# Output projection and MLP of a transformer block: products on pairs of 16-bit floats in place of fp32r pairs, with the MLP weights split once

## The chip, the cores and the metric

The kernel runs on one core of a Trainium2 chip. The metric is the device time of one execution in microseconds (us); the times of a kernel are given as the median of several runs. A core has TensorE (PE in the profile, its weight loads as PEld), VectorE (DVE), ScalarE (ACT), GpSimd (POOL) and SyncE (SP), which issues the DMAs here. Each engine works through its own instructions in order; semaphores tie them together.

## The reference

One pre-norm transformer block over S = 2048 rows of D = 512: softmax attention with 32 heads of 16, and an MLP with F = 1792 and SiLU. All inputs and the output are float32.

```
qkv = layernorm(x) @ wqkv
p   = softmax(q @ k.T / 4)            # 32 heads of 16
h   = x + concat(p @ v) @ wo
out = h + silu(layernorm(h) @ w1) @ w2
```

## The kernel before, in words

The kernel wants nearly float32 precision from matmuls on cheaper operands. It splits each operand into a high part and a rest ("low") and adds three products, high by high, low by high and high by low (`product`, L123). In the projections of q, k and v, the output projection and the MLP, both parts are of the type fp32r, a 4-byte type. The queries and keys, once projected, are pairs of 16-bit floats instead: `measure` (L454) finds a power of two from the sums of squares of the weights, so that nothing overflows, and `project_qk` (L468) scales and splits with it.

Time has these stages.

- **Projections** (to about 188 us in the profile). In units of one product (12 matmuls, `project_qk`, `project_v` L492) over four blocks of 512 rows; the last 24 units run in a loop over groups of heads (L661). ACT copies the result out of PSUM, scaled, POOL takes the rest, and SP stores q and k to DRAM (`qd`, `kd`). Two or three PSUM banks serve the products in turn.
- **Attention**. The loop at L1109 goes over 512 groups: 4 blocks of 512 queries x 8 items (four heads each) x 16 key chunks. A group has four score matmuls (`scores`, L400), ACT's four exponentials, and eight matmuls for the values of two groups before (`values`, L689). Softmax needs the maximum of each row of scores ahead of time; `maximum` (L245) makes a matmul of 48 rows into a PSUM bank and a DVE reduction, 64 per item. A planner (`maxima`, L1087) places up to three per group and the rest elsewhere: `burst` (L379) puts several at fixed steps of other products. The maxima and other work share three banks that are taken in turn (L677), and at times the bank `pv`.
- **Small chains beside it**: `finish_max` (L261) on DVE and POOL and `place_max` (L291) turn maxima into rows of the queries; `sums`, `invert`, `spread`, `divide` (L769 to L794) divide the attention output by its sums through DRAM, with POOL's slow power operation in `invert`. `soon` (L317) queues such a step some groups ahead.
- **Output projection** of a finished block (`output`, L946, in the first item of the next block): `split_rows` (L832) splits the rows, `project_rows` (L852) multiplies, then statistics, normalisation and transposes.
- **MLP** (`mlp`, L894): 14 steps over F in chunks of 128. A step has a first product with w1 (12 matmuls into `pv`), `gate` (L867: SiLU and cast on ACT, the rest `gl` on DVE) and the second product with w2 of the chunk before (`second`, L874: 12 matmuls into four accumulating banks). Bursts of 3, 3 and 4 maxima stand at steps 5 and 12 of the first product and 8 of the second (`BESIDE_C`, L74); the third block has none in its last three steps (`QUIET`, L78), the fourth none at all. The first three blocks' MLPs run this way between groups of attention.
- **The last block** (`finish_last`, L980) has its output projection and MLP in an order written out by hand.

The weight tiles of the MLP are loaded and split anew in each block: `load_weights` (L813) loads 128 x 512 float32, and `split_weights` (L821) casts the high part on ACT and takes the rest on POOL, or on DVE in the last block:

```
w = raw_w.pop((kind, f))
...
act("copy", wh, w)
...
low(wl, w, wh, engine)
```

Of the kernel before, what the change touches and what calls it, by code (L numbers as in the profile page):

```python
# [20 lines left out]
P = 128  # L21
# [14 lines left out]

TOP = 2.0 ** 15
MX = 2.0 ** 15

# [42 lines left out]
def attention_mlp_kernel(ctx: ExitStack, tc: tile.TileContext, x, wqkv, wo, w1, w2, out):  # L82
# [28 lines left out]
    def low(dst, src, high, engine="dve"):  # L111

        if engine == "pool":
            pool("tensor_tensor", dst, src, high.bitcast(F32), ALU.subtract)
        else:
            dve("tensor_tensor", dst, src, high.bitcast(F32), ALU.subtract)

# [34 lines left out]
    nc.vector.tensor_copy(ident_h, ident)  # L152
    expo = const.tile([P, 1], F32, name="expo")
    nc.gpsimd.memset(expo, -0.5)
    minus = const.tile([P, 16], F32, name="minus")
# [3 lines left out]
    qk_s = const.tile([P, 1], F32, name="qk_s")  # L159
    qk_e = const.tile([P, 1], F32, name="qk_e")  # L160

    fix_q = const.tile([16, 512], F16, name="fix_q")
# [12 lines left out]

    def statistics(rows):
# [6 lines left out]
        pool("tensor_scalar", rs, mv[:, 1:2], EPS, None, op0=ALU.add)  # L183
        pool("tensor_tensor", rs, rs, expo, ALU.pow)
        return mv, rs
# [226 lines left out]
    with ExitStack() as pa:  # L412
# [15 lines left out]
        scaled = ks[RING - 1].rearrange("p a n -> p (a n)").bitcast(F32).rearrange("p (t n) -> p t n", n=512)  # L428
        scaled = [scaled[:, t, :] for t in range(4)]
        flat = va.rearrange("p c h d -> p (c h d)")  # L430
# [7 lines left out]

        sq = small.tile([P, NG], F32, name="sq", bufs=1)

        def square(n):
# [26 lines left out]
        def project_qk(b, n, beside={}, scale=False, kind="st"):  # L468
# [9 lines left out]
            if scale:  # L478

                t = scaled[b]  # L480
# [94 lines left out]
        for t in range(4):  # L575
# [18 lines left out]
        for b in range(NB):  # L594
# [3 lines left out]
            for n, (kind, k) in enumerate(units + vs if b else units):  # L598
                tick()
                rows, (stats, norms, turns) = None, ((), (), ())  # L600
                if b + 1 < NB:
                    rows = xts[b + 1]
                    stats, norms, turns = (other_ln if b else first_ln)[n]

                def layer_norm():
                    for t in stats:
                        found[t] = statistics(rows[:, t, :])
                    for t in norms:
                        normalize(rows[:, t, :], rows[:, t, :], *found.pop(t), engine="pool" if kind == "v" else "dve")
# [74 lines left out]
    ot = [cpool.tile([P, 4, DC, P], F32, name=f"ot{i}") for i in range(2)]  # L684
    wo_h = cpool.tile([P, DC, D], F32R, name="wo_h")
    wo_l = cpool.tile([P, DC, D], F32R, name="wo_l")
    hth = cpool.tile([P, DC, 512], F32R, name="hth")
    htl = cpool.tile([P, DC, 512], F32R, name="htl")
    def values(g):  # L689
# [55 lines left out]
    def divide_part(part, pvs, o_t, kind="st"):  # L745
# [3 lines left out]
        halves = ps.rearrange("p t (m j r) -> p t m j r", m=2, r=32)[:, :, :, :, :DH + 1]  # L749
        both = gp.tile([P, 4, P], F32, name="both", tag="ol")[:, :, :2 * (DH + 1)].rearrange("p t (j r) -> p t j r", j=2)  # L750
# [3 lines left out]
        dve("reciprocal", rc, both[:, :, :, DH])  # L754
        to = o_t[:, :, 64 + 32 * part:96 + 32 * part].rearrange("p t (j d) -> p t j d", j=2)
        dve("tensor_tensor", to, both[:, :, :, :DH], rc[:, :, :, None].to_broadcast([P, 4, 2, DH]), ALU.mult)
# [17 lines left out]
    def invert(i):  # L774
# [4 lines left out]
        pool("tensor_tensor", x, x, rc, ALU.mult)  # L779
        pool("tensor_scalar", x, x, -1.0, 2.0, op0=ALU.mult, op1=ALU.add)  # L780
        pool("tensor_tensor", rc, rc, x, ALU.mult)
# [25 lines left out]

    raw_w, ws, hx, os = {}, {}, {}, {}


    first_weights = {9: ("w1", 0), 12: ("w1", 1), 14: ("w2", 0), 15: ("w1", 2)}

    def load_weights(kind, f):  # L813
        if f < FC:
            w = raw_w[kind, f] = gp.tile([P, 512], F32, tag="w", name="w", bufs=4)
            if kind == "w1":
                dma(w.rearrange("p (c n) -> p c n", n=P), w1[:, f * P:(f + 1) * P].rearrange("(c p) n -> p c n", p=P))
            else:
                dma(w, w2[f * P:(f + 1) * P, :])

    def split_weights(kind, f, engine, high="act", pt=False):  # L821
        if f < FC:
            w = raw_w.pop((kind, f))
            wh, wl = ws[kind, f] = [pt_tile(kind + part, F32R) if pt else gp.tile([P, 512], F32R, name=kind + part)
                                    for part in "hl"]
            if high == "act":
                act("copy", wh, w)
            else:
                dve("tensor_copy", wh, w)
            low(wl, w, wh, engine)  # L830

    def split_rows(b, t, chunks=slice(None)):  # L832
        if chunks.start != DC - 1:
            os[t] = [gp.tile([P, DC, P], F32R, name=name) for name in ("oh", "ol")]
        (h, l), o = (x[:, chunks] for x in os[t]), ot[b % 2][:, t, chunks]
# [6 lines left out]

    def split_wo(c, w):
        pool("tensor_copy", wo_h[:, c, :], w)
        low(wo_l[:, c, :], w, wo_h[:, c, :], "pool")
# [14 lines left out]
    def add_rows(b, t, ps):  # L860

        dve("tensor_tensor", rows_of(b, t), ps, hx[t], ALU.add)

    def turn_rows(t):
        turn(hx.pop(t), hth[:, :, t * P:(t + 1) * P], htl[:, :, t * P:(t + 1) * P])

    def gate(ps, engine="dve"):  # L867
        g, gh, gl = (pt_tile(name, dt) for name, dt in (("g", F32), ("gh", F32R), ("gl", F32R)))
        act("activation", g, ps, AF.Silu)
        act("copy", gh, g)  # L870
        low(gl, g, gh, engine)
        return gh, gl

    def second(b, acc, f, gh, gl, inserts={}):  # L874
# [8 lines left out]
        for t, step in enumerate(steps):  # L883
# [5 lines left out]
            for m in range(parts):  # L889
                cols = slice(m * D // parts, (m + 1) * D // parts)  # L890
                dve("tensor_tensor", h[:, cols], acc[t][:, cols], h[:, cols], ALU.add)
                dma(out[n * P:(n + 1) * P, cols], h[:, cols])

    def mlp(b):  # L894
# [10 lines left out]
        for f in range(FC):  # L905
# [21 lines left out]
            parts = gate(ps, "dve" if f else "pool")  # L927
            if f == FC - 1:
# [17 lines left out]
    def output(b, n):  # L946
# [13 lines left out]
        if n < 4:  # L960
            found[n] = statistics(rows_of(b, n))

# [17 lines left out]
    def finish_last(pending):  # L980
# [22 lines left out]
        def add(t):  # L1003
            h = rows_of(b, t)
            dve("tensor_tensor", h, ps_rows[t], hx[t], ALU.add)
            found[t] = statistics(h)

# [23 lines left out]

        split_weights("w1", 2, "dve", pt=True)
        some(1, 5)
# [24 lines left out]
        turn_second(3)  # L1058
        split_weights("w2", 0, "dve")
        for f in range(3):  # L1060
            begin(f, 1)
        acc, waiting = [], []
        for f in range(FC):
# [10 lines left out]
            waiting.append((f, *gate(ps)))  # L1074
            if f:
                split_weights("w1", f + 2, "dve")
            if f > 1:
                split_weights("w2", f - 1, "dve")
            if f > 1:
                second(b, acc, *waiting.pop(0))  # L1080
        split_weights("w2", FC - 1, "dve")
        while waiting:
# [26 lines left out]
    for g in range(groups):  # L1109
# [7 lines left out]
        if g < DC:  # L1117
            w = gp.tile([P, 512], F32, tag="w", name="w", bufs=4)
            dma(w, wo[g * P:(g + 1) * P, :])
            soon(8, split_wo, g, w)  # L1120
        if i in FIRSTS:
            b, n = i // 8 - 1, c - OUTPUT
# [10 lines left out]
            if c == 13:  # L1133
                split_weights("w1", 0, "pool")
        if i == LAST:
# [5 lines left out]
            if c == 4:  # L1141
                for f in range(3):
                    load_weights("w1", f)
                load_weights("w2", 0)
                for f in range(2):
                    soon(8 + f, split_weights, "w1", f, "dve", "dve")
        if g == 1:
# [64 lines left out]
```

## Time and profile before

| | |
|---|---|
| median of 3 runs | 1664.33 us (1663.91 to 1664.33) |
| span of the profiled execution | 1662.2 us; some 2 us of the run's time lie around it |
| projections | to about 188 us |
| MLP of the first block | from about 486 us, some 110 us |
| MLP of the last block | 1588 to 1657 us |
| DMA | 102.85 MB, 62 GB/s on average |

The profile has one execution. Its page gives the busy time of each engine, then groups of instructions by source line, engine, operation and tile: `out<-in`, partitions x elements and type, count, busy time in us and mean ns of one, idle time before and what ended it. fp32r operands show as f32 in matmul rows and as fp32r where an engine writes them. Timeline rows give start, duration, engine, line, operation, tiles and count; rows that follow one another are merged. Matmuls overlap in a pipeline, so a matmul's duration isn't its cost; the distance from one start to the next is. Helpers such as `mm` (L89), `act` (L103), `dve` (L106) and `pool` (L96) record all operations of an engine, so tiles tell the groups apart.

### The profile page before, as it was taken

What the parts mean: (1) busy time and instruction counts of PE and PEld (TensorE: products, weight loads), DVE (VectorE), ACT (ScalarE), POOL (GpSimd) and SP (SyncE); (2) the same over time, 40 slices, a digit from 0 to 9 for tenths busy, and PEclk for the clock granted to TensorE, in tenths of its full rate; (3) what the DMA queues carried; (4) which work ended last, traced back from release to release, by engine and by line L of the source; (5) the groups of instructions that cost most, each with busy time, mean ns of one, the idle gap of its engine ahead of it and who ended that gap; (6) DMA issues with size and microseconds to landing.
All of it is one profiled execution on the core that took longest, in us unless ns stands there. A gap on an engine that the chain in (4) does not pass through costs nothing.

```text
span 1662.2 us, 28571 instructions
## 1 busy us (share of the span) xinstructions
PE 1649.9 (99%) x10551; PEld 649.6 (39%) x10551; DVE 1454.3 (87%) x2403; ACT 1235.3 (74%) x2435; POOL 397.3 (24%) x584
## 2 busy tenths in 40 slices
PE   9999999999999999999999999999999999999999
PEld 7666422222245532222245532222245632222387
DVE  7899999999988889999988889999978769999443
ACT  5323799999953389999962379999962389999743
POOL 5423311211234301211244311211235311111100
PEclk9999999999999999999999999999999999999999
DMA  5434411211232111111232111121232211100222
GB/s 201 107 98 143 119 32 37 58 32 37 72 73 67 58 50 35 42 50 33 60 76 79 58 50 32 37 58 32 61 70 76 68 50 34 33 12 21 65 77 82
DMA packets 104409, 102.85 MB, mean 62 GB/s; under 512 B 22737, under 2 KB 81169, under 8 KB 104269
## 3 DMA queue, kind: packets, MB, share of 16 engines
q1 hardware_dynamic: 104268, 101.02, 22.4%
q8 instruction: 83, 1.36, 0.4%
q14 instruction: 58, 0.47, 0.1%
HBM read 77.72 MB, written 17.29 MB: 57 GB/s over the span
## 4 chain that ended last, share of the span: by engine, by line
PE 90%; DVE 5%; ACT 3%; issue 1%; POOL 0%; DMA 0%; DVEq 0%; POOLq 0%; ACTq 0%
PE pv L89 35%; PE ps_s L89 21%; PE ps_m L89 11%; PE ps_acc L89 10%; PE ps_qk L89 5%; PE ps_w L89 3%; DVE mx L257 3%; PE ps_v L89 3%; ACT pt L103 2%; PE ps_wo L89 2%; PE ps_tr L92 1%; DVE st L106 0%; DVE pvs L106 0%; DVE hx L106 0%; PE ps_n L92 0%
## 5 line engine op out<-in xcount | busy, mean ns | idle before, releaser
L257 DVE TENSOR_REDUCE mx<-ps_m 128x1 f32<-128x512 f32 x2011 | 1261.7, 684 | 80.8 <-PE ps_m L89 50.6
L103 ACT ACTIVATE pt<-ps_s 128x512 f32<-128x512 f32 x2048 | 1010.7, 608 | 31.9 <-PE ps_m L89 17.4
L89 PE MATMUL pv<-pt,va 128*17 128x512 f32 x4096 | 537.6, 598 | 0.9
L89 PE MATMUL ps_s<-qs,ks 64*128 64x512 f16 x2048 | 532.2, 379 | 2.0 <-ACT pt L103 0.6
L89 PE MATMUL ps_m<-ks,qs 48*128 48x512 f16 x2011 | 504.8, 380 | 0.7 <-DVE mx L257 0.2
L89 PEld LDWEIGHTS <-ks 64*128 64x128 f16 x2048 | 150.2, 95 | 548.1 <-issue 435.4
L96 POOL TENSOR_TENSOR ri<-rc,minus 128x16 f32<-128x16 f32 x31 | 90.8, 2928 | 305.8 <-DMA rc<-dn 305.8
L89 PEld LDWEIGHTS pv<-pt,va 128*17 128x17 f32 x4096 | 69.0, 95 | 215.0 <-issue 202.3
L89 PEld LDWEIGHTS <-qs 48*128 48x128 f16 x2048 | 119.2, 94 | 62.6 <-issue 56.7
L103 ACT CAST w2h<-w 128x512 fp32r<-128x512 f32 x56 | 34.7, 619 | 99.6 <-PE ps_acc L89 99.6
L103 ACT ACTIVATE g<-pv 128x512 f32<-128x512 f32 x39 | 23.3, 597 | 100.1 <-PE pv L89 100.1
L89 PE MATMUL ps_acc<-w2l,gh 128*128 128x512 f32 x224 | 92.6, 413 | 0.0
L89 PE MATMUL ps_acc<-w2h,gh 128*128 128x512 f32 x224 | 92.0, 411 | 0.0
L96 POOL TENSOR_TENSOR w2l<-w,w2h 128x512 fp32r<-128x512 f32 x42 | 53.9, 1284 | 147.9 <-ACT w2h L103 147.9
L89 PE MATMUL ps_acc<-w2h,gl 128*128 128x512 f32 x224 | 88.6, 396 | 0.0
L106 DVE TENSOR_TENSOR gl<-g,gh 128x512 fp32r<-128x512 f32 x53 | 37.3, 703 | 56.2 <-ACT gh L103 56.2
L103 ACT ACTIVATE ks<-ps_qk,qk_s 128x512 f32<-128x512 f32 x30 | 20.7, 689 | 68.8 <-PE ps_qk L89 66.9
L96 POOL TENSOR_SCALAR nm<-nm 128x16 f32<-128x16 f32 (+1 forms) x50 | 12.8, 255 | 232.7 <-DVE nm L268 229.7
L89 PE MATMUL pv<-htl,w1h 128*128 128x512 f32 x156 | 65.5, 420 | 0.0
L89 PE MATMUL pv<-hth,w1h 128*128 128x512 f32 x156 | 62.4, 400 | 0.1
L89 PE MATMUL pv<-hth,w1l 128*128 128x512 f32 x156 | 61.4, 393 | 0.0
L96 POOL TENSOR_TENSOR w1l<-w,w1h 128x512 fp32r<-128x512 f32 x42 | 54.3, 1292 | 11.3 <-ACT w1h L103 11.3
(138 smaller groups left out, 1396.3 us busy)
## 6 DMA issues: line engine op xcount, KB each, us to landing
w<-in_B_w_dram SPq DMA_DIRECT2D x112, 256.0 KB
ks<-kd SPq DMA_DIRECT2D x120, 192.0 KB
qs<-qd SPq DMA_DIRECT2D x128, 48.0 KB
kd<-sh SPq DMA_DIRECT2D x16, 256.0 KB
qd<-sh SPq DMA_DIRECT2D x16, 256.0 KB
hx<-in_A_x_dram SPq DMA_DIRECT2D x16, 256.0 KB
ot<-pvs SPq DMA_DIRECT2D x124, 32.0 KB
den<-dr SPq DMA_DIRECT2D x124, 32.0 KB
```

The source lines that it names most:

```text
L89: tc.keep_in_program_order(nc.tensor.matmul(*a, **k))
L92: tc.keep_in_program_order(nc.tensor.transpose(*a))
L96: tc.keep_in_program_order(getattr(nc.gpsimd, op)(*a, **k))
L103: pin(getattr(nc.scalar, fn)(*a, **k))
L106: pin(getattr(nc.vector, fn)(*a, **k))
L257: pin(nc.vector.tensor_reduce(mx[piece][:, j, a % n, qt, kb:kb + 1], ps, axis=AX.X, op=ALU.max))
```

## The change

- The operands of the output projection, of the first MLP product and of the second (`wo_h`, `wo_l`, `hth`, `htl`, w1, w2, `gh`, `gl`, the split rows) become pairs of 16-bit floats. The three products stay three, with the same counts and sizes. The projections of q, k and v stay on fp32r.
- So that 16-bit floats hold them, w1, w2, wo, the attention output and the gate are scaled by powers of two. They are found on the chip: during the projections SP loads w1, w2 and wo in 32 pieces of 128 x 512, ACT squares each with an accumulated sum (`square_rest`), and squares the value weights in one instruction (`square_values`); then one small matmul and small operations of DVE and POOL make the factors (`measure_rest`, `set_factors`). The staging takes two of the four `scaled` buffers of `project_qk`. The layer norm of the MLP scales its rows by 1024.
- The factors are taken out again in operations that are there anyway: the residual adds become operations with a scalar factor, SiLU takes a scale, the cast of the gate becomes a multiplication, and `gl` an operation with a scalar factor, always on DVE.
- w1 and w2 are split once: from group 12 of attention, every fourth group loads one of 28 tiles; four groups later POOL scales it, a group later casts it, another group later takes the rest, and SP stores the pair to DRAM (`wd`). In the MLPs `load_weights` loads the finished pair, in the same number of bytes. `split_weights` in its old form goes, with all its calls, and `split_wo` has one more POOL operation.

```diff
+        def square_rest(u):
+
+            n = u - 4
+            if 0 <= n < len(pieces):
+                act("activation", staged[n % 2], staged[n % 2], AF.Square, accum_out=rest_sq[:, n:n + 1])
+            n = u - 2
+            if 0 <= n < len(pieces):
+                dma(staged[n % 2], pieces[n])
...
+                square_values()
...
             for n, (kind, k) in enumerate(units + vs if b else units):
                 tick()
+                square_rest(2 + 6 * (b - 1) + n if b else n)
...
                 n = 8 * g + m - 12
+                square_rest(n + 24)
+                if n == 14:
+                    measure_rest()
+                if n == 16:
+                    set_factors()
...
     def load_weights(kind, f):
         if f < FC:
+            w = parts_of(raw_tile())
+            dma(w, wd[kind][f])
+            ws[kind, f] = w[:, 0], w[:, 1]
...
+    def split_weights(kind, f, w):
+
+        parts = parts_of(raw_tile())
+
+        def store():
+            low(parts[:, 1], w, parts[:, 0], "pool")
+            dma(wd[kind][f], parts)
+
+        pool("tensor_scalar", w, w, w1_s if kind == "w1" else w2_s, 1.0, op0=ALU.mult, op1=ALU.mult)
+        soon(1, lambda: pool("tensor_copy", parts[:, 0], w))
+        soon(2, store)
...
-        act("copy", gh, g)
-        low(gl, g, gh, engine)
-        return gh, gl
+    def gate(ps):
+        g, parts = pt_tile("g"), parts_of(pt_tile("gh"))
+        act("activation", g, ps, AF.Silu, scale=h_f)
+        act("mul", parts[:, 0], g, g_s)
+        dve("scalar_tensor_tensor", parts[:, 1], g, g_s, parts[:, 0], op0=ALU.mult, op1=ALU.subtract)
+        return parts[:, 0], parts[:, 1]
...
-            for kind, n in (("w2", f), ("w1", f + 1)) if f else (("w1", 1), ("w2", 0)):
-                split_weights(kind, n, "pool")
...
+        f, c4 = divmod(g - SPLIT, 4)
+        if c4 == 0 and 0 <= f < 2 * FC:
+            kind, f = ("w1", "w2")[f % 2], f // 2
+            soon(4, split_weights, kind, f, load_raw(kind, f))
```

More of the change, by code (lines that the diff above doesn't have):

```diff
@@ L37 @@
 TOP = 2.0 ** 15
+LN = 2.0 ** 10
+BOUND = 23.0
+PIECES = 14, 14, 4
+SPLIT = 12
 MX = 2.0 ** 15
@@ L111, in low @@
     def low(dst, src, high, engine="dve"):
[L113 to L116, printed above, removed]
+        if high.dtype == F32R:
+            high = high.bitcast(F32)
+        (pool if engine == "pool" else dve)("tensor_tensor", dst, src, high, ALU.subtract)
     def run(*parts):
@@ L160, in attention_mlp_kernel @@
     qk_e = const.tile([P, 1], F32, name="qk_e")
+    factors = const.tile([P, 14], F32, name="factors")
+    sigma, inverse = factors[:, :4], factors[:, 4:8]
+    w1_s, w2_s, wo_s, o_s = (sigma[:, n:n + 1] for n in range(4))
+    h_f, g_s, out_f, wo_f, o_minus, o_twice = (factors[:, n:n + 1] for n in range(8, 14))
     fix_q = const.tile([16, 512], F16, name="fix_q")
@@ L174, in attention_mlp_kernel, with statistics @@
     dr = dram.tile([H, 4, 512], F32, name="dr")
-    def statistics(rows):
+    wd = {kind: dram.tile([FC, P, 2, 512], F16, name=f"{kind}d") for kind in ("w1", "w2")}
+    def statistics(rows, scale=1.0):
         st = small.tile([P, 6], F32, name="st", bufs=5)
@@ L428, in attention_mlp_kernel @@
         scaled = ks[RING - 1].rearrange("p a n -> p (a n)").bitcast(F32).rearrange("p (t n) -> p t n", n=512)
-        scaled = [scaled[:, t, :] for t in range(4)]
+        scaled, staged = ([scaled[:, t, :] for t in half] for half in ((0, 1), (2, 3)))
         flat = va.rearrange("p c h d -> p (c h d)")
@@ L439, in attention_mlp_kernel, with square_values, measure_rest, set_factors @@
         sq = small.tile([P, NG], F32, name="sq", bufs=1)
+        free = qs[RING - 1].rearrange("p a n -> p (a n)").bitcast(F32)
+        rest_sq, norms = free[:, :sum(PIECES) + 1], free[:, 64:68]
+        pieces = [w.rearrange("(p r) f -> p (r f)", p=P)[:, 512 * n:512 * (n + 1)]
+                  for w, count in zip((w1, w2, wo), PIECES) for n in range(count)]
+        def square_values():
+            act("activation", ks[RING - 1].rearrange("p a n -> p (a n)").bitcast(F32).rearrange(
+                "p (c n) -> p c n", n=512), raw_v, AF.Square, accum_out=rest_sq[:, sum(PIECES):])
+        def square_rest(u):
[5 more added lines that the diff above has]
+                dma(staged[n % 2], pieces[n])
+        def measure_rest():
+            n = sum(PIECES)
+            ps = bank("ps_sq", "sm")
+            mm(ps[:, :n + 1], ones, rest_sq, start=True, stop=True)
+            dve("tensor_reduce", norms[:, :2], ps[:, :28].rearrange("p (a k) -> p a k", a=2), axis=AX.X, op=ALU.add)
+            dve("tensor_reduce", norms[:, 2:3], ps[:, 28:n], axis=AX.X, op=ALU.add)
+            dve("tensor_copy", norms[:, 3:4], ps[:, n:n + 1])
+            pool("tensor_scalar", norms, norms, 1e-30, None, op0=ALU.add)
+            pool("tensor_tensor", norms, norms, expos, ALU.pow)
+        def set_factors():
+            dve("tensor_scalar", sigma[:, :3], norms[:, :3], TOP, None, op0=ALU.mult)
+            dve("tensor_scalar", sigma[:, 3:], norms[:, 3:], TOP / BOUND, None, op0=ALU.mult)
+            dve("tensor_scalar", sigma.bitcast(U32), sigma.bitcast(U32), 0x7F800000, None, op0=ALU.bitwise_and)
+            dve("reciprocal", inverse, sigma)
+            for to, a, f in ((h_f, inverse[:, :1], 1 / LN), (g_s, w1_s, 1 / 32.0), (o_minus, o_s, -1.0),
+                             (o_twice, o_s, 2.0), (out_f, inverse[:, :1], 32.0)):
+                pool("tensor_scalar", to, a, f, None, op0=ALU.mult)
+            pool("tensor_tensor", out_f, out_f, inverse[:, 1:2], ALU.mult)
+            pool("tensor_tensor", wo_f, inverse[:, 2:3], inverse[:, 3:], ALU.mult)
         def square(n):
@@ L478, in project_qk @@
             if scale:
-                t = scaled[b]
+                t = scaled[b % 2]
                 act("mul", t, ps, qk_s)
@@ L684, in attention_mlp_kernel @@
     ot = [cpool.tile([P, 4, DC, P], F32, name=f"ot{i}") for i in range(2)]
[L685 to L688, printed above, removed]
+    wo_h = cpool.tile([P, DC, D], F16, name="wo_h")
+    wo_l = cpool.tile([P, DC, D], F16, name="wo_l")
+    hth = cpool.tile([P, DC, 512], F16, name="hth")
+    htl = cpool.tile([P, DC, 512], F16, name="htl")
     def values(g):
@@ L805, in split_half, with raw_tile, parts_of, load_raw @@
         low(l, o, h)
-    raw_w, ws, hx, os = {}, {}, {}, {}
+    ws, hx, os = {}, {}, {}
     first_weights = {9: ("w1", 0), 12: ("w1", 1), 14: ("w2", 0), 15: ("w1", 2)}
+    def raw_tile():
+        return gp.tile([P, 512], F32, tag="w", name="w", bufs=8)
+    def parts_of(w):
+        return w.bitcast(F16).rearrange("p (s n) -> p s n", s=2)
     def load_weights(kind, f):
         if f < FC:
[L815 to L830, printed above, removed]
+            w = parts_of(raw_tile())
+            dma(w, wd[kind][f])
+            ws[kind, f] = w[:, 0], w[:, 1]
+    def load_raw(kind, f):
+        w = raw_tile()
+        if kind == "w1":
+            dma(w.rearrange("p (c n) -> p c n", n=P), w1[:, f * P:(f + 1) * P].rearrange("(c p) n -> p c n", p=P))
+        else:
+            dma(w, w2[f * P:(f + 1) * P, :])
+        return w
+    def split_weights(kind, f, w):
[6 more added lines that the diff above has]
+        soon(2, store)
     def split_rows(b, t, chunks=slice(None)):
         if chunks.start != DC - 1:
-            os[t] = [gp.tile([P, DC, P], F32R, name=name) for name in ("oh", "ol")]
+            parts = gp.tile([P, 2, DC, P], F16, name="oh")
+            os[t] = parts[:, 0], parts[:, 1]
         (h, l), o = (x[:, chunks] for x in os[t]), ot[b % 2][:, t, chunks]
@@ L1058, in finish_last @@
         turn_second(3)
-        split_weights("w2", 0, "dve")
         for f in range(3):
```

46 lines of the change are left out of this document (18 added, 28 removed).

## The prediction

> **What bounds the kernel now.** I read the head of the page first, then the chain that ended last, then the busy time by stretches, then the timeline of one stretch.
>
> ```profile
> span 1662.2 us, 28571 instructions
> PE 1649.9 (99%) x10551; PEld 649.6 (39%) x10551; DVE 1454.3 (87%) x2403; ACT 1235.3 (74%) x2435; POOL 397.3 (24%) x584
> PE 90%; DVE 5%; ACT 3%; issue 1%; POOL 0%; DMA 0%; DVEq 0%; POOLq 0%; ACTq 0%
> ```
>
> PE carries 90% of the chain. A busy PE says little, so the question by stage is how far apart its matmuls start, and which engine would be late if they came closer. In the rows by stretches below, the columns are the stretch, its length, then PE, PEld, DVE, ACT and POOL busy, the granted clock, the DMA share and GB/s. The four are the projections, attention, ten steps of the first block's MLP, and the last block's MLP.
>
> ```profile
> 100.00:150.00 50.00, 50.00 (x242) 30.91 (x241) 48.81 (x82) 17.35 (x29) 19.53 (x32) 1.00 0.52 149
> 300.00:400.00 100.00, 99.76 (x766) 22.41 (x765) 95.86 (x158) 99.85 (x204) 16.56 (x29) 1.00 0.17 42
> 500.05:577.78 77.73, 77.69 (x341) 46.03 (x341) 68.52 (x111) 23.59 (x40) 30.73 (x34) 1.00 0.22 67
> 1588.76:1656.23 67.47, 67.47 (x292) 54.71 (x292) 23.43 (x37) 27.00 (x48) 0.00 (x0) 1.00 0.25 79
> ```
>
> An MLP step of the first three blocks takes 7.77 us (77.73 / 10). ACT works 2.36 us of it and POOL 3.07, so the weight splits that the change takes from them are hidden there. DVE works 6.85, so only 0.92 us per step is slack. In the last block DVE is busy a third of the time, and PE alone sets the pace.
>
> **Part 1: the matmuls.** These are the groups by shape of the third matmul of each product, each standing for three groups of equal count:
>
> ```profile
> L89 PE MATMUL ps_acc<-w2h,gl 128*128 128x512 f32 x224 | 88.6, 396 | 0.0
> L89 PE MATMUL pv<-htl,w1h 128*128 128x512 f32 x156 | 65.5, 420 | 0.0
> L89 PE MATMUL ps_w<-htl,w1h 128*128 128x512 f32 x56 | 22.1, 394 | 0.0
> L89 PE MATMUL ps_w<-htl,w1h 128*128 128x256 f32 x24 | 3.8, 280 | 0.0
> L89 PE MATMUL ps_wo<-wo_h,oh 128*128 128x512 f32 x48 | 20.5, 426 | 0.6
> L89 PE MATMUL ps_wo<-wo_h,hth 128*128 128x512 f32 x16 | 6.7, 421 | 0.0
> ```
>
> That makes 3 x (224 + 156 + 56 + 48 + 16) = 1500 matmuls of 512 columns and 72 of 256 that change from fp32r to 16-bit operands. Their durations overlap; the cost of one is the distance of starts. From the chain in order of time (start, length, what):
>
> ```profile
> 1579.12 1.42 PE ps_w L89 x12
> 1588.76 2.81 PE ps_acc L89 x12
> 1647.12 2.80 PE ps_w L89 x12
> ```
>
> From 1588.76 to 1647.12 lie 21 groups of twelve, so one takes 58.36 / 252 = 0.2316 us (0.118 at 256 columns). No full 128-row matmul on 16-bit operands is in this trace. The nearest are the scores and maxima of attention, on 64 and 48 rows, 16-bit, 512 columns:
>
> ```profile
> 442.04 0.39 PE L89 MATMUL ps_s<-qs,ks 64*128 64x512 f16 x1
> 444.00 0.39 PE L89 MATMUL ps_s<-qs,ks 64*128 64x512 f16 x1
> 444.23 0.59 PE L89 MATMUL ps_s<-qs,ks 64*128 64x512 f16 x2
> 444.67 0.38 PE L89 MATMUL ps_s<-qs,ks 64*128 64x512 f16 x1
> ```
>
> The pair at 444.23 spans 0.59 and one spans 0.38, so the step is 0.21; from 444.45 (the second of the pair) to 444.67 it is 0.22. I take 0.216 for the full matmul too; the bounds are 0.21 and, if the full array gains nothing, 0.2316. The gain is 1500 x 0.0156 = 23.4 us, and 72 x 0.008 = 0.6.
>
> The Trainium skill (TensorE: Matmul & The Clock Gate, Weight-path perf modes) says that the array takes one element per cell and cycle whatever its width, and that a weight load goes by columns, not bytes. By that, this part would gain nothing. These rows of the weight loads stand against it, 188 ns against 95 for the same 128 columns, as 0.2316 against 0.216 does:
>
> ```profile
> L89 PEld LDWEIGHTS ps_acc<-w2h,gl 128*128 128x128 f32 x224 | 42.1, 188 | 9.4 <-issue 1.1
> L89 PEld LDWEIGHTS <-ks 64*128 64x128 f16 x2048 | 150.2, 95 | 548.1 <-issue 435.4
> ```
>
> **Part 2: coming back from a burst of maxima.** A weight load behind a running matmul is hidden, but after a change of rows it isn't. One burst in an MLP step, the next ones, and DVE's answer:
>
> ```profile
> 522.44 0.39 PE L89 MATMUL pv<-hth,w1l 128*128 128x512 f32 x1
> 522.76 0.60 PE L89 MATMUL ps_m<-ks,qs 48*128 48x512 f16 x3
> 523.29 0.50 PE L89 MATMUL pv<-htl,w1h 128*128 128x512 f32 x1
> 523.63 0.39 PE L89 MATMUL pv<-hth,w1h 128*128 128x512 f32 x1
> 525.12 0.60 PE L89 MATMUL ps_m<-ks,qs 48*128 48x512 f16 x3
> 527.72 0.60 PE L89 MATMUL ps_m<-ks,qs 48*128 48x512 f16 x3
> 525.54 1.89 DVE L257 TENSOR_REDUCE mx<-ps_m 128x1 f32<-128x512 f32 x3 [0.47 <-PE ps_m L89]
> 527.35 0.68 DVE L106 TENSOR_TENSOR gl<-g,gh 128x512 fp32r<-128x512 f32 x1
> 528.14 0.69 DVE L257 TENSOR_REDUCE mx<-pv 128x1 f32<-128x512 f32 x1
> ```
>
> The first fp32r matmul after the burst holds the next one back by 0.34 (523.29 to 523.63), where the 16-bit scores, just returned from the values, take 0.23 (444.00 to 444.23). The wait into the burst (0.32) I leave as it is, less the shorter step. So each return saves 0.11, of which 0.016 is counted in part 1. Returns, from the code: two per product in 14 + 14 + 11 steps, 78; in the second products 15 + 15 + 13; in the output projections 4, and 12 more entries from scores: 137 x 0.094 = 12.9 us. Parts 1 and 2 together are 36.9 us. The end of the output projection has waits of its own on normalisation and transposes; I take off 0.5.
>
> **Part 3: what is late next, DVE.** Without other waits a step would fall to 7.77 - 24 x 0.0156 - 3 x 0.094 = 7.11. DVE must do ten maxima at a distance of 0.60 ((1.89 - 0.68) / 2) and gl, and the maxima have three rotating banks beside pv. Two places become tight. (a) The burst of four (527.72): DVE starts 0.42 later, and its fourth maximum ends 0.42 + 3 x 0.60 + 0.69 = 2.91 after the burst. The next burst comes 2.82 after it (522.76, with the burst of four one step earlier at 519.95), and its third matmul, 0.22 on, needs that same bank: at 3.04 it is free, but nine matmuls and one return sooner, at 2.81, it isn't. PE waits some 0.15. (b) gl becomes an operation with a scalar factor; the nearest row is
>
> ```profile
> L106 DVE SCALAR_TENSOR_TENSOR sl<-ps_qk,qk_s,sh 128x512 f16<-128x512 f32 x2 | 1.5, 752 | 1.3 <-ACT sh L103 1.3
> ```
>
> so 0.07 longer than 0.68. From the burst at 525.12 DVE needs 0.42 + 3 x 0.60 + 0.67 = 2.89; the burst of four has its data at 2.60 + 0.42 = 3.02 now, and at 2.80 then. DVE starts it 0.1 late, which (a) passes on to PE. Together 0.26 per step: 7.37 instead of 7.11. In 12 + 12 + 9 steps this returns 8.6 us, with the ends of the blocks about 10. The last block has no maxima and keeps all.
>
> **Part 4: what is added.** In the projections ACT squares 32 pieces of w1, w2 and wo, one per unit, and the value weights in one long instruction. On POOL each of the 28 weight tiles is scaled, cast and subtracted in the first block's attention, and stored.
>
> ```profile
> 0.72 2.62 DMA ks<-in_A_x_dram
> 146.60 2.98 PE ps_qk L89 x12
> 150.34 2.98 PE ps_qk L89 x12
> L103 ACT ACTIVATE qs<-va 128x512 f32<-128x512 f32 x8 | 5.1, 632 | 0.2
> L103 ACT ACTIVATION_READ_ACCUMULATOR qs<-va 128x1 f32 x8 | 1.5, 188 | 0.0
> L96 POOL TENSOR_SCALAR ks<-ks,mv,rs 128x512 f32<-128x512 f32 x4 | 8.8, 2202 | 0.0
> L96 POOL CAST wo_h<-w 128x512 fp32r<-128x512 f32 x4 | 2.5, 616 | 6.4 <-PE ps_m L89 6.4
> L96 POOL TENSOR_TENSOR wo_l<-w,wo_h 128x512 fp32r<-128x512 f32 x4 | 5.1, 1282 | 0.3
> ```
>
> A unit lasts 3.74 (146.60 to 150.34). A square with its read costs 0.82; ACT is busy 17.35 of 50 there, 1.3 per unit, so it fits into idle time, as long as its piece has landed. The load is issued two units ahead (7.5 us) and 256 KB landed in 2.62 at the start. On SP's queue the load waits for the square of two pieces before; the unit's stores and key loads stand behind it, and they wait for ACT and POOL of the same unit anyway. The long square, four times 0.63 at most, stands ahead of three copies that free banks for the first key product: 0.7 us on the path, 2.5 at most. The scale factors are some seven small DVE instructions of about 0.17 where DVE is busy 48.81 of 50: 1.2 us. I count 2.
>
> POOL's 2.20 + 0.62 + 1.28 = 4.1 us fall on every fourth group of attention, 7.84 us (four times 442.04 to 444.00), above its 16.56 per 100: about 70% busy. Behind it wait the inversion of sums, whose result is needed only at the block's end, the placing of maxima, mostly many groups ahead, and SP's stores. DVE's maxima read PSUM. The cost lies between nothing and one group's stall per item (8 x 2 us); I take 0.5, near nothing, because POOL isn't on the chain. The scaling of Wo adds 4 x 2.2 on POOL before anything waits for it. In the MLP the loads from DRAM keep their number and size and come one or two steps ahead.
>
> **The sum.** 36.9 - 0.5 - 10 - 2.5 = 23.9. The profiled execution spans 1662.2, and the median of the runs, 1664.33, is 2.1 above; I carry that over: 1662.2 + 2.1 - 23.9, **1640 us**.
>
> **Rivals.** (1) *DVE doesn't bite*: the bank wait is met by slack that I can't see. Then part 3 falls away, and the additions may be hidden wholly: 1664 - 37 = 1627. For it: DVE's 6.85 is below 7.11. Against: the two places worked out. Chance 0.18. (2) *The full array steps at 0.2316*, and only the returns shorten: 12.9 - 2.5, so 1664.3 - 10.4 = 1654. The 64-row rows are for a smaller array, so this can't be excluded: 0.10. (3) *16-bit operands do nothing at all*, step and weight load alike: no gain, the 2.5 of part 4, and 0.07 of gl that stays in DVE's slack: 1667. Against: the load rows, 95 ns; 0.04. By this rule of width the named page of the Trainium skill would stand. (4) *The squares hold the projections*, and it ends slower: if a piece lands later than two units after its issue, ACT waits on it, and behind it the copy that frees the projection's bank, so PE stops. At a landing of 10.8 us the unit becomes about 5.4 instead of 3.74, 28 units cost 46 us: 1686. It decides from some 9.2 us of landing, where the units lose the 24 us gained. For it: DMA share 0.52 already, and SP's order. Against: 2.62 us at the start, when the rates are highest. Chance 0.06. (5) *POOL's or ACT's additions cost more, yet less than the gain*: one stall of 2 us per item and the long square whole, 1640 + 8 x 1.5 = 1652: 0.10. My own case keeps 0.52.
>
> **Range and chances.** The range must hold the first case, (1), (2) and (5), and leaves out (3) and (4): 1625 to 1654. A difference of 0.2%, 3.3 us, is about what a measurement of this kernel tells from none. Faster: 0.52 + 0.18 + 0.10 + 0.10 = 0.90, less 0.02 for errors of several at once, 0.88. Within 0.2%: 0.04, out of (3) and that margin. Slower: 0.08.
>
> **What would show it.** Part 1: groups of twelve in the last block at 2.59 instead of 2.80. Part 2: 0.23 instead of 0.34 after a burst. Part 3: MLP steps of 7.3 to 7.4, and PE waiting for DVE mx where there is almost no such wait now; steps of 7.1 would mean (1), 7.5 (2). Part 4: key units still 3.74 apart, attention groups of the first block still 1.96; longer units with ACT waiting for a DMA into its staging tile would mean (4). Wrong altogether would be a DVE that is slowed by the mixed operands of gl: at 1 us more it would set every step.

## The result, and the profile after

The changed kernel takes 1649.0 us (median of 4 runs, 1646.65 to 1649.58); the kernel before took 1664.33 on the same chip. The ratio is 0.9905, with a 95% interval of 0.9891 to 0.9919. The profiled execution took 1649.26 and spans 1647.5, that is 14.7 less than before. The time lies inside the range, but 9 us above the 1640 predicted: the kernel won 15 us where 24 were forecast.

The head of the page and the chain that ended last, after:

```profile
span 1647.5 us, 28474 instructions
PE 1624.0 (99%) x10553; PEld 516.1 (31%) x10553; DVE 1439.0 (87%) x2385; ACT 1206.6 (73%) x2391; POOL 363.5 (22%) x594
PE 79%; DVE 14%; ACT 4%; DMA 2%; issue 1%; POOL 0%; SPq 0%; DVEq 0%; ACTq 0%
```

PE's weight loads fell from 649.6 to 516.1 us. On the chain, DVE rose from 5% to 14%, and DMA, which had nothing there, has 2%. Both are clues: the first to the MLP steps, the second to the loss.

Next, the stages. The first two rows give the matmuls of the values before and after, with the first start and the last; the third gives the output projections after. Then follow the rows by stretches (columns as in the prediction) of the first block's attention, before and after.

```profile
L89 PE MATMUL pv<-pt,va x4096: 590/593/606, 188.3 to 1564.5; 128*17 128x512 f32 x196
```
```profile
L96 PE MATMUL pv<-pt,va x4096: 590/593/607, 201.4 to 1555.0; 128*17 128x512 f32 x196
L96 PE MATMUL ps_wo<-wo_h,oh x96: 376/379/390, 469.8 to 1227.2; 128*128 128x512 f16 x96
```
```profile
188.30:456.90 268.60, 267.87 (x2039) 59.98 (x2039) 257.03 (x419) 268.31 (x547) 54.01 (x87) 1.00 0.21 51
```
```profile
201.40:469.80 268.40, 267.79 (x2039) 59.97 (x2039) 256.72 (x418) 268.11 (x547) 125.93 (x175) 1.00 0.39 106
```

The projections end at 201.4 instead of 188.3. The first block's attention is as long as before, 268.5, though POOL works 126 us there instead of 54. From the first matmul of an output projection to the last of the MLP, worked out from the starts of the matmuls in both traces:

| Stage | before | after | difference |
|---|---|---|---|
| projections, to the first matmul of the values | 188.3 | 201.4 | +13.1 |
| attention of the first block | 268.6 | 268.5 | -0.1 |
| output projection and MLP, block 1 | 139.0 | 131.5 | -7.5 |
| block 2 | 139.0 | 131.5 | -7.5 |
| block 3 | 132.6 | 125.1 | -7.5 |
| last block, to the last MLP matmul | 92.9 | 87.5 | -5.4 |

So the 16-bit products gained 27.9 us, and the projections gave 13.1 of them back. Everything else is where it was, to 0.2 us.

**The MLP steps.** A step of the first block in the rows by stretches, and its timeline:

```profile
520.15:527.49 7.34, 7.27 (x37) 2.44 (x36) 6.82 (x11) 1.41 (x2) 0.00 (x0) 1.00 0.28 71
```
```profile
522.38 0.74 DVE L113 SCALAR_TENSOR_TENSOR gh<-g,factors,gh 128x512 f16<-128x512 f32 x1
522.52 0.60 PE L96 MATMUL ps_m<-ks,qs 48*128 48x512 f16 x3
...
523.64 3.77 DVE L271 TENSOR_REDUCE mx<-ps_m 128x1 f32<-128x512 f32 x6
523.93 0.59 PE L96 MATMUL pv<-hth,w 128*128 128x512 f16 x2
524.36 0.38 PE L96 MATMUL pv<-htl,w 128*128 128x512 f16 x1
524.57 0.59 PE L96 MATMUL pv<-hth,w 128*128 128x512 f16 x2
525.10 0.83 PE L96 MATMUL ps_m<-ks,qs 48*128 48x512 f16 x3
525.87 0.39 PE L96 MATMUL pv<-htl,w 128*128 128x512 f16 x1
526.09 0.59 PE L96 MATMUL pv<-hth,w 128*128 128x512 f16 x2
```

7.34 instead of 7.77. The return from a burst costs 0.22 to the next start (525.87 to 526.09), not 0.34. The burst at 525.10 lasts 0.83 where the others take 0.60: its third matmul comes 0.23 late, while DVE runs through six maxima without a pause. In the trace it starts at 525.56, just after DVE goes from one maximum to the next (525.53), so I read it as a wait for a bank that DVE was still reading; the list of waits doesn't name it.

**The last block**, from its chain in order of time:

```profile
1604.54 2.59 PE ps_acc L96 x12
1607.13 2.59 PE ps_w L96 x12
...
1633.03 2.59 PE ps_w L96 x12
```

Twelve matmuls take 2.59, that is 0.216 each.

**The loss.** From each unit's first matmul I took its start in both traces. The lag of after behind before is 1.1 us from the first key product (22.7) to 38; at 48.6 it is 6.9, at 54.5 8.9, at 67.5 11.1, at 72.5 11.7; then it grows only to 13.1 by the end. So 10.6 us of the 13.1 arise between 38 and 72 us, in the second block of the projections. The timeline of that stretch (SP's, ACT's, DVE's and PE's rows, others left out):

```profile
40.07 0.42 SPq L116 DMA_DIRECT2D ks<-in_B_w_dram  x1
...
41.58 0.46 SPq L116 DMA_DIRECT2D ks<-in_A_x_dram  x1
42.09 0.56 SPq L116 DMA_DIRECT2D ks<-in_B_w_dram  x1
...
43.04 0.63 ACT L110 ACTIVATE ks<-ks 128x512 f32<-128x512 f32 x1 [5.38 <-DMA ks<-in_B_w_dram]
43.66 0.57 ACT L110 COPY va<-ps_v 128x512 f32<-128x512 f32 x1
44.13 0.59 ACT L110 CAST xth<-ps_tr 128x512 fp32r<-128x512 f32 x1
44.71 6.70 SPq L116 DMA_DIRECT2D ks<-kd  x8
44.75 0.69 DVE L113 TENSOR_TENSOR xtl<-ps_tr,xth 128x512 fp32r<-128x512 f32 x1 [5.69 <-ACT xth L110]
45.36 4.86 DVE L271 TENSOR_REDUCE mx<-ps_m 128x1 f32<-128x512 f32 x8
46.09 1.78 PE L96 MATMUL ps_m<-ks,qs 48*128 48x512 f16 x3 [3.87 <-DVE mx L271]
...
49.96 0.63 ACT L110 ACTIVATE ks<-ks 128x512 f32<-128x512 f32 x1 [5.24 <-DMA ks<-in_B_w_dram]
```

Read it from the bottom up. PE waits 3.87 for DVE's maxima; DVE had stood 5.69 waiting for ACT's cast `xth`; ACT had stood 5.38 waiting for the first piece of weights, so that the square could run, with the copy and the cast behind it. And SP issued that piece's load only at 40.07, 2.4 after ACT had begun to wait for it (43.04 less 5.38). Sixteen loads of queries and keys went out before it, from 32.59 on, one each 0.46 us. The second piece is issued at 42.09, behind a load of 1 MB of rows, and lands at 49.93: here the transfer itself is long, and the chain that ended last runs through it. Then eight key loads hold SP from 44.71 to 51.41, and the third piece is issued at 51.50. The eight issues take only 3.2 of these 6.7 us. For most of the rest SP waits until the load of rows has landed; in the trace the fifth key load and that load carry the same one of eight semaphores, which SP's loads and stores take in turn. The row of the chain, and that of SP's waits up to 205 us (sum, times, longest; the 2.6 is the one here):

```profile
42.09 7.84 DMA ks<-in_B_w_dram
```
```profile
SPq L116 <- DMA ks<-in_A_x_dram: 3.4, 3, 2.6
```

### The profile page after: what moved, and what is told of

Read it like the earlier page. It is cut to its first block, busy times and chain, and to the rows that moved or that the text cites. A ratio compares the mean times of both kernels' runs of the same rounds, so it can differ in the third digit from the quotient of the medians.

```text
span 1647.5 us, 28474 instructions
## 1 busy us (share of the span) xinstructions
PE 1624.0 (99%) x10553; PEld 516.1 (31%) x10553; DVE 1439.0 (87%) x2385; ACT 1206.6 (73%) x2391; POOL 363.5 (22%) x594
## 2 busy tenths in 40 slices
DMA packets 100951, 125.91 MB, mean 76 GB/s; under 512 B 24144, under 2 KB 61072, under 8 KB 100812
## 4 chain that ended last, share of the span: by engine, by line
PE 79%; DVE 14%; ACT 4%; DMA 2%; issue 1%; POOL 0%; SPq 0%; DVEq 0%; ACTq 0%
PE pv L96 32%; PE ps_s L96 21%; DVE mx L271 11%; PE ps_m L96 10%; PE ps_qk L96 5%; PE ps_acc L96 4%; PE ps_w L96 3%; ACT pt L110 3%; PE ps_wo L96 2%; PE ps_v L96 2%; DVE gh L113 1%; DMA ks<-in_B_w_dram 1%; PE ps_tr L99 1%; DVE ot L113 0%; DVE pvs L113 0%
## 5 line engine op out<-in xcount | busy, mean ns | idle before, releaser
L110 ACT ACTIVATE pt<-ps_s 128x512 f32<-128x512 f32 x2048 | 1010.4, 608 | 30.0 <-PE ps_m L96 17.8
L110 ACT ACTIVATE g<-pv,factors 128x512 f32<-128x512 f32 x39 | 26.8, 688 | 217.5 <-PE pv L96 217.5
L96 PE MATMUL ps_acc<-w,gh 128*128 128x512 f16 x672 | 161.2, 380 | 0.0
L113 DVE SCALAR_TENSOR_TENSOR gh<-g,factors,gh 128x512 f16<-128x512 f32 x56 | 41.7, 745 | 63.7 <-ACT gh L110 63.7
L96 PEld LDWEIGHTS <-w 128*128 128x128 f16 x708 | 65.2, 98 | 93.6 <-issue 29.1
L96 PE MATMUL pv<-hth,w 128*128 128x512 f16 x312 | 92.9, 379 | 0.0
L96 PEld LDWEIGHTS <-gh 128*128 128x128 f16 x672 | 59.2, 98 | 95.1 <-issue 32.4
L96 PE MATMUL pv<-htl,w 128*128 128x512 f16 x156 | 59.5, 381 | 0.0
L103 POOL TENSOR_SCALAR nm<-nm 128x16 f32<-128x16 f32 (+1 forms) x50 | 13.1, 261 | 198.7 <-DVE nm L282 195.7
L96 PE MATMUL ps_qk<-xth,wqk_h 128*128 128x512 f32 x128 | 53.6, 419 | 0.6 <-ACT va L110 0.6
L96 PE MATMUL ps_qk<-xth,wqk_l 128*128 128x512 f32 x128 | 50.7, 396 | 0.0
L103 POOL TENSOR_TENSOR sl<-ks,sh 128x512 f16<-128x512 f32 x30 | 34.8, 1161 | 70.4 <-ACT sh L110 56.9
```

The costliest lines, as they stand in the source:

```text
L96: tc.keep_in_program_order(nc.tensor.matmul(*a, **k))
L103: tc.keep_in_program_order(getattr(nc.gpsimd, op)(*a, **k))
L110: pin(getattr(nc.scalar, fn)(*a, **k))
L113: pin(getattr(nc.vector, fn)(*a, **k))
```

## The experiments

My theory: *the place of the piece loads in SP's queue* makes the squares late, and ACT's order hands that on. Rivals: ACT's added work by itself; the added transfers, which fill the DMA engines. A question of its own is whether DVE keeps the MLP steps from falling further.

**Loads and squares six units later.** Both start a block later, when the sixteen loads are out.

```diff
-                square_rest(2 + 6 * (b - 1) + n if b else n)
+                square_rest(2 + 6 * (b - 2) + n if b > 1 else 0)
...
-                square_rest(n + 24)
+                square_rest(n + 18)
```

(`measure_rest` and `set_factors` move to the last two units.)

> All loads and squares of w1, w2 and wo come six units later: the first load stands in the third block of the projections instead of the second, the factors are found in the last two units. Theory (queue): the changed kernel loses 10.5 us in the second block because the first pieces' loads stand on SP behind sixteen query and key loads, and ACT holds back copies that PE needs while it waits for them. Then the projections end about 10 us earlier, and the time is 1638 to 1640 against 1649. Rival (transfer rate): 8 MB of loads cost PE time wherever they stand; then 1649. Rival (ACT work): the squares themselves are too much for ACT in a unit; then also 1649, since as many squares stand in as tight units.

Measured 1639.1 us, ratio to before 0.9849 (0.9833 to 0.9866). The projections end at 190.5, 2.2 behind before instead of 13.1, and the other stages are as in after. All of the loss but 2 us depends on where the loads and squares stand.

**The first four squares left out, the loads left in** (the factors lack those sums; the work of these pieces on ACT goes).

```diff
-            if 0 <= n < len(pieces):
+            if 4 <= n < len(pieces):
                 act("activation", staged[n % 2], staged[n % 2], AF.Square, accum_out=rest_sq[:, n:n + 1])
```

> The squares of the first four pieces are left out (their part of the sums of w1 is wrong), their loads stay. In the second block ACT then waits for no piece. Queue theory: the second block of the projections gets its 10.5 us back, 1638 to 1640. Rival (transfer rate): the loads still take bandwidth from the key and query loads and the rows of x; 1647 to 1649. Rival (ACT work): four squares of 0.82 us go, so at most 3.3 us: 1646.

Measured 1643.9 us, ratio 0.9877 (0.986 to 0.9893), so the time is missed by 4 us. The second block got its time back: until 53 us the lag is 0.7, though the DMA engines are 0.92 busy from 42 to 48. So the transfers alone don't hurt PE. But the loss came back later. Its timeline:

```profile
44.33 8.73 SPq L116 DMA_DIRECT2D ks<-kd  x8
53.10 0.42 SPq L116 DMA_DIRECT2D ks<-in_B_w_dram  x1
...
60.96 0.63 ACT L110 ACTIVATE ks<-ks 128x512 f32<-128x512 f32 x1 [10.56 <-DMA ks<-in_B_w_dram]
```

The fifth square, the first left in, waits 10.56 us: the loads ahead of its own are still queued behind the eight key loads. The projections end 9.3 behind before. I had expected SP to have caught up by then. The loss moves with the first square that stands ahead of ACT's other work while SP is behind.

**The first six loads left out, the squares left in** (they square what is in the buffer, so the factors come from other data).

```diff
-            if 0 <= n < len(pieces):
+            if 6 <= n < len(pieces):
                 dma(staged[n % 2], pieces[n])
```

> The loads of the first six pieces are left out, their squares stay and take what lies in the buffers (the sums are wrong). Queue theory: no wait for a DMA in the second block, about 10 us back, 1638 to 1641. Rival (ACT work): the squares are all there, so nothing comes back, 1649. Rival (transfer rate): as the queue theory, 1639; the run with loads alone tells these two apart.

Measured 1638.87 us, ratio 0.9847 (0.983 to 0.9863). The same squares without a wait cost next to nothing. ACT's added work is ruled out as the cause.

**The loads issued by ACT instead of SP**, with after's timing:

```diff
-                dma(staged[n % 2], pieces[n])
+                pin(nc.scalar.dma_start(staged[n % 2], pieces[n]))
```

> The kernel after with its timing, only the twenty-nine loads of pieces issued by ScalarE instead of SyncE. If the stall in the second block of the projections comes from the place of the loads in SyncE's order (behind sixteen loads of queries and keys, then eight of keys that hold SyncE 6.7 us), the squares no longer wait and the run takes 1639 to 1642. Rival: the transfers themselves are slow there because the DMA engines are 0.85 to 0.92 busy from 42 to 60 us; then the pieces land late whichever queue issues them, and it takes 1644 to 1649.

Measured 1638.29 us, ratio 0.9842 (0.9827 to 0.9858). ACT issues all 32 loads here (the expectation says twenty-nine). The run separates SP's order from full DMA engines. The rows by stretches from 42 to 54 us, first of after, then of this kernel, and this kernel's row of the eight key loads, then its load of the second piece and its first square:

```profile
42.00:48.00 6.00, 2.10 (x5) 0.41 (x4) 3.25 (x6) 1.68 (x4) 1.11 (x1) 0.84 0.89 264
48.00:54.00 6.00, 6.00 (x20) 4.32 (x19) 2.98 (x6) 1.68 (x4) 0.00 (x0) 0.59 0.70 228
```
```profile
42.00:48.00 6.00, 6.00 (x34) 4.13 (x31) 5.43 (x10) 3.10 (x7) 0.92 (x1) 1.00 0.96 245
48.00:54.00 6.00, 6.00 (x29) 3.81 (x28) 5.15 (x10) 2.21 (x7) 1.28 (x1) 1.00 0.71 231
```
```profile
44.88 8.99 SPq L116 DMA_DIRECT2D ks<-kd  x8
```
```profile
32.60 0.33 ACTq L471 DMA_DIRECT2D ks<-in_B_w_dram  x1
...
37.36 0.63 ACT L110 ACTIVATE ks<-ks 128x512 f32<-128x512 f32 x1
```

The DMA engines are busier than in after (0.96 against 0.89), the key loads hold SP even longer (8.99), and yet PE issues 34 and 29 matmuls where after had 5 and 20. The same bytes, loaded at the same units from another queue, go out some 10 us earlier (the second piece at 32.60 instead of 42.09) and land in time. A slow transfer is there too: the load issued at 44.36 has its last packet at 51.64, 7.3 us later, and PE doesn't feel it. So an early issue is enough; how much of after's loss is the late issue, and how much the long transfer behind it, no run separates. ACT's waits for DMAs up to 205 us (sum, times, longest): in after a row for the pieces, in this kernel none for them, but one that the list puts to the load of rows:

```profile
ACT ks L110 <- DMA ks<-in_B_w_dram: 23.4, 10, 5.4
```
```profile
ACT va L110 <- DMA ks<-in_A_x_dram: 3.2, 1, 3.2
```

The last is ACT, at 48.24, held before it can issue a load of its own, whose semaphore is that of the load of rows. PE doesn't lose by it: the lag behind before is 1.2 at the units around it.

The Trainium skill (Trainium Kernel Development and Optimization, Key Constraints) says that DMAs issued from several engines run on the same DMA engines, and that issuing from more than one saves only the sequencer's issue time. Nothing here speaks against it: the bytes are the same 125.91 MB, and the DMA engines are no less busy. But what ACT's queue spares a load is the place behind SP's other loads and SP's waits, and that is worth 10.7 us here.

**`gl` on POOL.** For the DVE limit of the MLP steps: ACT scales g in place and casts it, POOL takes the rest (in the last block the rest stays on DVE).

```diff
-        act("mul", parts[:, 0], g, g_s)
-        dve("scalar_tensor_tensor", parts[:, 1], g, g_s, parts[:, 0], op0=ALU.mult, op1=ALU.subtract)
+        act("mul", g, g, g_s)
+        act("copy", parts[:, 0], g)
+        low(parts[:, 1], g, parts[:, 0], engine)
```

> In the first three blocks the rest of the gate goes from DVE to POOL: ACT scales the gate in place (0.7 us) and casts it (0.62 us), POOL subtracts (1.2 us). The last block keeps the subtraction on DVE. Theory (two tight places on DVE): the steps of 7.34 us lose the part that gl causes, 0.11 us, and keep the wait for the maxima's bank, so 7.2 to 7.25 us and some 4 us in all: 1645. Rival (PE alone sets the step at 7.34): no change, 1649. Rival (DVE's total work sets it): DVE falls by 0.67 us, so steps fall to PE's 7.1 and the time by 8 us, to 1641.

Measured 1648.57 us, ratio 0.9907 (0.989 to 0.9923): not to be told from after, and 3.6 above the 1645 expected. The steps did fall as expected, from 7.34 to 7.25, but the first two blocks gained only 0.5 us each, the third 0.15, and the last lost 0.4. My reading: in the last step of a block no product stands between the gate and its second product, so the longer chain through ACT and POOL lies on the path. The run "All together" tests that.

**The long square behind the casts.** The loads six units later, and the square of the value weights moved behind the two casts of the next block's rows.

```diff
                 for n in (*keys[3:], *range(0, NG, 2)):
                     square(n)
-                square_values()
         turned = [turn_high(1, t) for t in range(2)]
+        square_values()
```

> The loads and squares six units later (as in the first experiment, 1639.1 us), and the long square of ScalarE (2.0 us at 20 us) moved behind the two casts that turn the second block's first rows. If the long square holds PE up there, as the lag of 1.1 us from the first key product on says, the projections end some 0.6 to 1.1 us earlier and the run takes 1638.0 to 1638.6. Rival: something after it waits instead (the casts are short of time anyway), then 1639 again.

Measured 1638.29 us, ratio 0.9844 (0.983 to 0.9857), against 1639.1 without the move. The times have the size forecast, but their ranges overlap, and the lag at the end of the projections differs by 0.2 us only. That comparison is blurred: at the last product of the values ahead of the square (17.8 us in before) the lag is already 0.1 in one trace and 0.5 in the other. From there to the first key product it grows by 0.50 with the square in its old place and by nothing without, and the chain no longer passes through ACT there. So the square costs some 0.5 us, a little under the 0.6 to 1.1 forecast.

**All together**: the run before, with `gl` on POOL in every step of the first three blocks but each block's last.

```diff
-            parts = gate(ps)
+            parts = gate(ps, "pool" if f < FC - 1 else "dve")
```

> As the run before, and gl made by POOL from a scaled copy of g in the steps of the three MLP blocks, except in the last step of each block; the last block keeps DVE's form. If the 0.65 us that the blocks lost when all steps were on POOL came from the last step's longer chain (which nothing covers), the steps' gain stays whole: 33 steps of 0.085 us are 2.8 us, and the run takes about 1635.5 (1635.0 to 1636.0). Rival: the loss lies in the first step or in VectorE's maxima elsewhere; then the gain is 0.5 us a block as before, and it takes 1636.5 to 1637.

Measured 1634.89 us, ratio 0.9824 (0.9811 to 0.9838): a little below the range expected, and the best of all. The blocks fall by 1.2, 1.2 and 0.8 us, more than twice what they gained with all steps on POOL, so the last step's chain had been the loss. Two rows of this kernel, a step by stretches and its tight burst:

```profile
508.33:515.58 7.25, 7.25 (x35) 2.44 (x35) 6.25 (x11) 2.03 (x3) 1.16 (x1) 1.00 0.00 0
```
```profile
513.29 0.75 PE L96 MATMUL ps_m<-ks,qs 48*128 48x512 f16 x3
```

DVE works 6.25 in the step instead of 6.82, and the burst still lasts 0.75, 0.15 too long.

## Why the prediction was right or wrong

**Part 1, right.** A full 128-row matmul on 16-bit operands steps at 0.216, as taken from the 64-row scores, and at 0.109 with 256 columns (0.118 before). Rivals (2) and (3) fall. With them falls the use that the prediction tried of the Trainium skill's rule of width (TensorE: Matmul & The Clock Gate, Weight-path perf modes), which that section states in comparing 8-bit with 16-bit types: it doesn't carry over to fp32r. At equal columns, 16-bit operands are faster than fp32r here, in the array (216 against 232 ns) and in the load:

```profile
L96 PEld LDWEIGHTS <-gh 128*128 128x128 f16 x672 | 59.2, 98 | 95.1 <-issue 32.4
```

98 ns against 188.

**Part 2, right.** The first matmul after a burst holds the next back by a median of 0.226 instead of 0.340 (start to start in both traces). I had left the way into a burst alone; it fell by a further 0.01 to 0.02.

**Part 3, right.** Steps of 7.34, forecast 7.37, where 7.11 would have meant that DVE doesn't bite. Its two places were found: with (b), `gl`, gone from DVE, the step falls by 0.09 (forecast 0.1) to 7.25, and the 0.15 of (a), the bank wait, is what remains of the distance to 7.11. Parts 1 to 3 were forecast at 26.4 together and gave 27.9; of the difference, 33 steps of 7.34 instead of 7.37 are 1.0, and the rest isn't traced.

**Part 4, POOL: right in sign, too careful.** I counted 0.5, and attention lost nothing. One term was well off: the scaling of a weight tile on POOL, in the first block's attention,

```profile
L103 POOL TENSOR_SCALAR w<-w,factors 128x512 f32<-128x512 f32 x32 | 22.3, 695 | 26.1 <-DMA w<-in_B_w_dram 17.8 <-PE pv L96 6.2 <-DMA den<-dr 2.1
```

takes 0.70 where I took 2.20. The row that I used has two scalar operands from SBUF, this one has one; whether that is the reason no run shows. Rival (5)'s 1652 doesn't follow from its terms either: one stall of 2 us per item and the whole long square, in place of the 0.5 and 0.7 counted, make 1657, outside the range.

**Part 4, the projections: wrong, and the whole miss.** I counted 2 us; they cost 13.1. The other parts came out 2.0 better than counted, which leaves the 9 us. That 1649 lies inside the range is luck: the range was widened for rivals (2) and (5), a slow array and stalls of POOL, and neither happened. The step that failed reads: "The load is issued two units ahead (7.5 us) and 256 KB landed in 2.62 at the start." Two units ahead in the program isn't two units ahead on SP. I named what stands *behind* the load in SP's queue and not what stands *ahead* of it: the sixteen loads of queries and keys at 0.46 us each, the 1 MB of rows, and the eight key loads, which hold SP for 6.7 us. The first piece was issued 2.4 us after ACT was ready for it. The second half of the sentence failed too: the second piece took 7.84 to land, three times as long. The experiments show it: without the loads, or with the loads a block later, or with the loads on another queue, some 10 us or more come back, and without the squares that wait for them the loss goes to the next square.

It is rival (4)'s mechanism, a landing later than two units, then square, copy behind it, PE, at a point that I had not thought of. I priced it as a rate that would hold in all 28 units (46 us, 0.06) or not at all. It came as a backlog in one block: from the third block on ACT waits a little for pieces, and PE loses 0.1 us by 148 us. My own case and rival (4) were both priced by an average over the stage, DMA share 0.52, where the 42 to 48 us row of before already had 0.85.

Of the other 2.5 us, 1.1 lies ahead of the first key product. Of that, 0.7 arises where the long square (2.0 us, on the chain of after) stands, as I took; the other 0.4 is there before it and varies from run to run: kernels with the same instructions up to there have 0.1 to 0.8. The remaining 1.4 comes late: 0.7 in the unit that starts at 148.6, where ACT waits 1.15 for a piece and the burst of maxima is 0.7 longer than in the kernel with ACT's queue, the rest in the last units with the factors. I took 1.2 for the factors; which of these is the cause is not shown.

## What to carry to other kernels

When a step is inserted with a load, write down the issuing queue's own order at that place, with the duration of each issue and what it waits for, and ask what stands ahead of the new load; a distance in units of work means nothing to a queue that is behind. An optional instruction with a wait, put ahead of the copies that free a busy engine's buffers, can cost what its wait costs, however short its work is: give it data that is long there, or another place. And a gain that frees the first engine shows up as less than itself where the second was near its limit, which the timeline of one step tells to a tenth of a microsecond.

## What the runs showed of the hardware

The stall cost more than itself, because TensorE's granted clock fell. In the two rows of after above, the clock is 0.84 and then 0.59, and PE, busy for all of the 6 us from 48 on, issues 20 matmuls where before it issued 29. The timeline of after:

```profile
49.14 0.63 PE L96 MATMUL ps_v<-wv_h,xtl 128*128 128x512 f32 x1
49.56 0.63 PE L96 MATMUL ps_v<-wv_l,xth 128*128 128x512 f32 x1
...
52.55 0.57 PE L96 MATMUL ps_v<-wv_h,xth 128*128 128x512 f32 x1
52.95 0.40 PE L96 MATMUL ps_v<-wv_h,xtl 128*128 128x512 f32 x1
53.19 0.39 PE L96 MATMUL ps_v<-wv_l,xth 128*128 128x512 f32 x1
```

From 49.14 to 52.55 the matmuls start 0.43 apart (3.41 us for eight), twice the usual 0.23; then the clock is back. The lag grew by 2.0 us over this unit (6.9 to 8.9), so about a fifth of the 10.6 is the slow clock after the wait and not the wait. The kernel with the first four squares left out shows it again: PE waits 4.95 us there, up to 62.31, the granted clock is 0.59 from 60 to 66 us, matmuls start 0.43 apart from 62.90 to 67.17, and the lag grows by 2.1 over that unit. In the traces' record of the clock, half speed lasts 6.83 us both times, from 46.08 and from 61.12. The Trainium skill (TensorE: Matmul & The Clock Gate, Part 1: The HAM clock gate (the "warmup" mystery)) says that the clock halves after an idle window of about 3.4 us and is restored after at least one busy window of that length. The trace agrees with the halving: PE stood still for 3.87 us and 4.95 us. It took longer to come back than one window: full speed returned 6.8 us after PE began again at 46.09, and in the other kernel 5.6 us after 62.31. In this kernel a stall of that length is to be priced with some 2 us on top.
